# The first pair's 32x32 systems: relaid on chip in place of four hops over DRAM, with a new order of the work

## The chip, the cores and the metric

One core of one Trainium2 chip runs the whole kernel. The metric is device time in microseconds of one execution, as the median of several runs. Engines are called as the profile calls them: PE (TensorE), DVE (VectorE), ACT (ScalarE), POOL (GpSimd), SP (SyncE, which here only issues transfers).

## The reference, cut to what matters

Three parts follow one another on 4 x 768 = 3072 tokens: a delta-rule attention with 8 heads of 48, a rational MLP (called MoE in the code), and eight experts with a capacity of 384 tokens each.

```python
# attention, per batch and head; state is 48x48
k_n = k / (norm(k) + 1e-06)
for t in range(768):
    y[t] = q[t] @ state
    state = state + beta[t] * outer(k_n[t], v[t] - k_n[t] @ state)
# rational MLP on x = y, 3072 x 384
h = x @ w_in                                   # 384 -> 2048
P = a[0] + a[1]*h + a[2]*h**2 + a[3]*h**3
Q = 1.0 + abs(b[0])*abs(h) + abs(b[1])*h**2
x2 = (P / (Q + 1e-06)) @ w_out                 # 2048 -> 384
# experts: greedy assignment of tokens by logits, then per expert
logits = x2 @ w_gate
out[mask] = maximum(x2[mask] @ w1[e], 0) @ w2[e]
```

The weights come in as 64-bit floats; the kernel decodes them to 32 bits on DVE and splits them into two halves of 16 bits.

## The kernel before

**Tiling.** The 768 positions are cut into 12 chunks (NCK) of 64. In a chunk the recurrence becomes a triangular system of 64x64 for each of the 32 heads (two halves of 16, U = 16, on 128 partitions). Each such system is solved in 32x32 blocks: two diagonal blocks and one block below them. Two chunks form a pair: pair 0 is chunks 0 and 1, pair 1 is chunks 2 and 3. A pair has 128 diagonal systems, one on each partition, 32x32 = 1024 numbers in the free dimension.

**How a pair's systems are made.** `gram` computes k k^T on PE into PSUM (tile tg). `gram_k` evacuates it to SBUF (tile ka; for chunk 1 the tile of xs) and writes it to DRAM (dA). `subst` loads it from there in the other layout, one system on a partition (pmA, eight transfers a pair), takes the norms from the diagonal (`root`, `nrec`), and inverts by columns (`col`, two instructions a column: a product into pmT, a subtraction in pmW). For pair 0 the columns run on VectorE and only up to 16x16 (n16: 15 columns on both 16x16 halves at once); the others run on POOL with 31 columns. The result is written to DRAM (dW) and read back by `inv_in` in the first layout (D). `parts` reads from dA the 16x16 blocks below the diagonal (F) and the 32x32 block (P). `merge(c)` completes the 32x32 inverse of a chunk from D and F: two runs of 128 small matmuls (`prod`), a transposition on VectorE, a copy, a subtraction. So the data of pair 0 go over DRAM at four places: dA written, read as pmA and as F and P, dW written, read as D.

**What follows.** The inverse of chunk 0 and P go through `comb`, `comb2`, `tr`, `y` and `pack` and give xT, the input of the MoE part. Each chunk is cut into 8 units: `h` (18 matmuls, line 875, with w_in), `s1`, `s2`, `s3` (the rational function on ACT, DVE and POOL), `x2` (12 matmuls, line 824, with w_out). Units 0 to 15 (chunks 0 and 1) are in the prologue, beside the decode of w_in (`wi_piece`, twelve pieces) and w_out (`wo_piece`, sixteen pieces); the first units need the first column block of w_in, the later ones the others, one after another. From unit 16 on the steady loop runs, then the last chunk, the routing and the experts.

**What sets the order.** `prologue` adds work to a list (`Sched`), each piece with its engine, an estimated time, the names that it reads and writes, and a priority (PP; in the loop LP); a lower priority goes first. `Sched.run` plans the list once, when the program is built, and emits the instructions in the planned order; on the chip every engine takes its instructions in that fixed order and waits by semaphores. All transfers named here are issued by SP, in order. Between the planned matmuls `run` puts warm-up matmuls (`hot`, line 1395) so that PE does not idle.

## Time and profile before

| | |
|---|---|
| time before, median of 3 runs | 968.44 us (965.59 to 973.08) |
| the profiled execution's own time | 968.31 us |
| its span on the core | 966.5 us |
| busy, share of the span | PE 88%, DVE 80%, ACT 58%, POOL 42% |
| DMA, mean over the span | 101 GB/s; 78336 of 101512 packets under 512 B |

The shares are means over stages with different limits, so the rows below are read by stage. Warm-up matmuls count as PE's busy time. A line number is one of the kernel before; "[4.45 <-DMA x]" behind an instruction is the idle time of its engine before it and what ended it. In a row of a stretch the engines stand in the order PE, PEld (weight loads), DVE, ACT, POOL. PEclk is the granted clock of PE as a share of full speed.

### The profile page before, as it was taken

The page shows a single profiled execution, that of the slowest core. Times are in us where ns is not written, and L with a number is a line of the kernel's source. Part 1 is how long each engine was busy: PE and PEld are TensorE (multiplying, and loading weights), DVE is VectorE, ACT ScalarE, POOL GpSimd, SP SyncE. Part 2 cuts the span into 40 slices and gives each one's busy share as a digit, 9 for nine tenths or more (in the row PEclk, how much of TensorE's full clock was granted, in tenths as well). Part 3 has the DMA queues.
Part 4 walks back from the last instruction along what each step waited for, and adds up shares of the span by engine and source line. Part 5 has one row for each costly group of instructions (what it writes and reads, how often), then busy time and mean ns, then how long its engine had stood idle before and what let it go on. Part 6 is the DMA issues. An engine that isn't in the chain of part 4 may idle for free.

```text
span 966.5 us, 30502 instructions
## 1 busy us (share of the span) xinstructions
...
## 2 busy tenths in 40 slices
...
GB/s 305 186 241 121 128 113 113 53 74 23 146 121 52 56 122 100 63 57 156 38 91 51 54 55 1 34 5 14 2 169 159 151 30 196 156 155 128 266 25 24
DMA packets 101512, 97.50 MB, mean 101 GB/s; under 512 B 78336, under 2 KB 86144, under 8 KB 98560
## 3 DMA queue, kind: packets, MB, share of 16 engines
...
q8 instruction: 101, 1.65, 0.8%
...
## 4 chain that ended last, share of the span: by engine, by line
PE 32%; DVE 29%; ACT 11%; DMA 10%; issue 10%; POOL 4%; SPq 3%; POOLq 0%; DVEq 0%; ACTq 0%
PE ph L875 9%; PE eph L770 4%; PE px L824 4%; DVE q L864 3%; DVE w L867 3%; DVE w L868 3%; PE px L783 3%; PE px L1395 3%; DVE w L851 2%; ACT q L858 2%; DVE q L850 2%; DMA xg<-x2d,perm 2%; DVE w L852 2%; ACT w L861 2%; DMA w1f<-in_moe_w_dram,ix 2%
## 5 line engine op out<-in xcount | busy, mean ns | idle before, releaser
L875 PE MATMUL ph<-xT,wi 128*128 128x256 f16 x1656 | 202.7, 278 | 26.4 <-DVE w L851 24.1
L875 PEld LDWEIGHTS <-wi 128*128 128x128 f16 x1728 | 167.0, 100 | 71.5 <-DVE w L851 34.6
L824 PE MATMUL px<-wo,gg 128*128 128x392 f16 (+1 forms) x1116 | 203.5, 333 | 5.2 <-ACT gg L840 2.9
L824 PEld LDWEIGHTS <-gg 128*128 128x128 f16 x1116 | 106.4, 99 | 75.0 <-issue 5.0
L841 POOL TENSOR_TENSOR gg<-w,gg 128x512 f16<-128x512 f32 x59 | 70.5, 1194 | 181.8 <-ACT gg L840 139.4
L188 POOL TENSOR_TENSOR pmW<-pmW,pmT 128x31 f32<-128x31 f32 (+15 forms) x155 | 94.9, 612 | 11.1
L187 POOL TENSOR_TENSOR pmT<-pmW,pmA 128x31 f32<-128x31 f32 (+15 forms) x155 | 86.6, 559 | 11.4
L861 ACT ACTIVATE w<-ph,cf 128x512 f32<-128x512 f32 x88 | 68.2, 775 | 22.8 <-PE ph L875 20.3
L867 DVE TENSOR_TENSOR w<-w,ph 128x512 f32<-128x512 f32 x88 | 59.8, 681 | 22.4 <-ACT q L858 12.2
L852 DVE SCALAR_TENSOR_TENSOR w<-q,w 128x512 f32<-128x512 f32 x88 | 76.5, 869 | 1.3
L840 ACT ACTIVATE gg<-w 128x512 f16<-128x512 f32 x88 | 55.4, 630 | 37.8 <-DVE w L852 37.3
L864 DVE SCALAR_TENSOR_TENSOR q<-q,cf,ph 128x512 f32<-128x512 f32 x88 | 65.1, 740 | 12.4 <-ACT w L861 6.8
L858 ACT ACTIVATE q<-ph,cf 128x512 f32<-128x512 f32 x88 | 60.0, 682 | 23.3 <-PE ph L875 12.7
L783 PEld LDWEIGHTS <-rr 128*128 128x128 f16 x576 | 52.3, 97 | 33.6 <-issue 2.3
L868 DVE SCALAR_TENSOR_TENSOR w<-w,cf,ph 128x512 f32<-128x512 f32 x88 | 65.3, 742 | 9.9 <-ACT q L858 9.4
L1395 PEld LDWEIGHTS <-warm 128*128 128x128 f16 x542 | 54.1, 104 | 24.5 <-issue 10.5
L773 ACT ACTIVATE rr<-eph 128x384 f16<-128x384 f32 x64 | 31.0, 490 | 60.3 <-PE eph L770 52.4
L850 DVE SCALAR_TENSOR_TENSOR q<-q,ph 128x512 f32<-128x512 f32 x88 | 59.8, 680 | 6.9 <-ACT ph L849 6.4
L865 ACT ACTIVATE q<-q 128x512 f32<-128x512 f32 x88 | 55.2, 628 | 16.9 <-DVE q L864 15.9
L851 DVE SCALAR_TENSOR_TENSOR w<-w,cf,ph 128x512 f32<-128x512 f32 x88 | 65.0, 738 | 0.0
L848 ACT ACTIVATE ph<-q,cf 128x512 f32<-128x512 f32 x88 | 60.6, 688 | 6.4 <-DVE ss L103 2.8
L788 POOL DMA_INDIRECT out_dram<-yo,perm x24 | 28.1, 1170 | 81.9 <-ACT yo L785 75.0
...
## 6 DMA issues: line engine op xcount, KB each, us to landing
...
```

The source lines that it names most:

```text
L187: if half==0: eng.tensor_tensor(t,W[:,0:r,j:j+1].to_broadcast([n,r,k]),A[:,j:j+1,j+1:32].to_broadcast([n,r,k]),op=OP.mult)
L188: else: eng.tensor_tensor(W[:,0:r,j+1:32],W[:,0:r,j+1:32],t,op=OP.subtract)
L783: g.add(('PE',.163,lambda P=P,rh=rh,wh=wh,f=f,part=part,i=i: nc.tensor.matmul(P,r[:,rh,f,128*i:128*i+128],W2[:,wh,f],start=(f,part)==(0,0) ...
L824: te.matmul(T['px',un//8][bp][:,0:O.N],gg()[:,gh,i,128*bp:128*bp+128],M.wo[:,wh,fb,0:O.N],start=fb==0 and n==0,stop=fb==15 and n==2,skip_g ...
L851: add(('DVE',.07+.6*z,lambda: ve.scalar_tensor_tensor(w(),w(),cf[:,0:1],y(),op0=OP.add,op1=OP.mult)),W+Y,W,un+O.pd('w3',un))
L852: add(('DVE*',.07+.535*z,lambda: ve.scalar_tensor_tensor(w(),q(),2.0,w(),op0=OP.subtract,op1=OP.mult)),Q+W,W,un+O.pd('w4',un))
L861: ac.activation(w(),P(),AF.Identity,bias=cf[:,2:3],scale=cf[:,3:4])
L864: add(('DVE',.07+.6*z,lambda: ve.scalar_tensor_tensor(q(),q(),cf[:,4:5],P(),op0=OP.add,op1=OP.mult)),Q+Pn,Q,un+O.pd('mu',un))
L867: add(('DVE',.07+.535*z,lambda: ve.tensor_tensor(w(),w(),P(),op=OP.mult)),W+Pn,W,un+O.pd('w1',un))
L868: add(('DVE',.07+.6*z,lambda: ve.scalar_tensor_tensor(w(),w(),cf[:,1:2],P(),op0=OP.add,op1=OP.mult)),W+Pn,W,un+O.pd('w2',un))
L875: for wh,xh in ((0,0),(0,1),(1,0)): te.matmul(T['P',un][:,i],M.wi[:,wh,part,128*fb:128*fb+128],xT()[:,xh,part],start=n==0,stop=n==8); n+=1
L1395: for _ in range(n): nc.tensor.matmul((bk['px1'] if t is None else t)[:,0:256],warm[:,0:128],warm,start=True,stop=True)
```

## The change

For pair 0 only, the four passages over DRAM go.

- `gram_0` replaces `gram_k` for chunks 0 and 1. The gram of chunk 0 goes to tg, that of chunk 1 to rec. Four evacuations a chunk (32 partitions each, 512 numbers, on ACT or DVE as the planner chooses) write the diagonal blocks of both chunks into one tile G (128x1024), with 32 numbers between neighbours; one stream transposition of G on VectorE gives pmA.
- F and P are evacuated from PSUM by ACT (`off`, four a chunk, scaled by s.odd, which is 1 on the partitions of the odd 16-row blocks and 0 elsewhere; `top`, two a chunk). s.odd is made by one small reduction at the start. `parts` and `inv_in` go.
- At the end of `subst` a second stream transposition, strided on both sides, writes the inverses of both chunks into one new tile nd (nd0, nd1), which replaces h4 and n0 as D.
- The planner's constants PP and LP are all new (cut here to those that the text speaks of).

```diff
--- before.py
+++ after.py
@@ -57,6 +57,7 @@
         nc.vector.tensor_scalar(s.ident,jp,0.0,None,op0=OP.is_equal)
         s.id16=c.tile([128,128],F16,name="id16"); nc.vector.tensor_copy(s.id16,s.ident)
         s.mask=c.tile([128,1,64],F32,name="mask")
+        s.odd=c.tile([128,1],F32,name="odd"); nc.vector.tensor_reduce(s.odd,s.ident.rearrange("t (a b x) -> t a b x",b=2,x=16)[:,:,1],axis=AX.XY,op=OP.add)
 
         s.dA=[[dr.tile([128,U,64],F32,name=f"dA{i}{j}") for j in range(2)] for i in range(2)]
         s.dW=[dr.tile([2,2,2,U,32,32],F32,name=f"dW{i}") for i in range(2)]
@@ -110,9 +111,9 @@
         eng.tensor_tensor(t,t,n[:,u,None].to_broadcast([128,u.stop-u.start,48]),op=OP.mult)
 
 
-    def gram(s,a,x,sw):
+    def gram(s,a,x,sw,pool=None):
         nc=s.nc
-        g=s.tg.tile([128,2,8,64],F32,name="tg")
+        g=(pool or s.tg).tile([128,2,8,64],F32,name="tg")
         for p in range(8):
             if s.mid and p%3==2: s.mid()
             for z in range(2):
@@ -121,12 +122,22 @@
                     t=64*(h^(sw*(p//4))); nc.tensor.matmul(g[t:t+64,r,p],a[o,p,h],x[o,p,h],start=True,stop=True)
         return g
 
-    def gram_k(s,c,ka=None):
+    def gram_0(s,c,P,F):
+        nc=s.nc; k=s.kT[c]; g=s.gram(k,k,0,s.rec if c else s.tg)
+        def out(i,act=True):
+            o=slice(32*i,32*i+32); b=32*(i%2); y=s.G.rearrange("t (x c p r) -> t c r p x",x=32,c=2,p=8)[o,c]; x=g[o,:,:,b:b+32]
+            if act: nc.scalar.activation(y,x,AF.Copy)
+            else: nc.vector.tensor_copy(y,x)
+        def off(i): o=slice(32*i,32*i+32); b=32*(i%2); nc.scalar.activation(F[o].rearrange("t (p r) x -> t r p x",r=2)[:,:,:,0:16],g[o,:,:,b:b+16],AF.Copy,scale=s.odd[o])
+        def top(h): o=slice(64*h,64*h+32); nc.scalar.activation(P[o].rearrange("t (p r) x -> t r p x",r=2),g[o,:,:,32:64],AF.Copy)
+        s.pend+=[lambda act=True,i=i: out(i,act) for i in range(4)]+[lambda i=i: off(i) for i in range(4)]+[lambda h=h: top(h) for h in range(2)]
+
+    def gram_k(s,c):
         nc=s.nc; k=s.kT[c%4]
         g=s.gram(k,k,0)
-        t=[ka]
+        t=[None]
         def out(act=True):
-            if ka is None: t[0]=s.wk.tile([128,U,64],F32,name="ka")
+            t[0]=s.wk.tile([128,U,64],F32,name="ka")
             o=t[0].rearrange("t (p r) x -> t r p x",r=2)
             if act: nc.scalar.activation(o,g,AF.Copy)
             else: nc.vector.tensor_copy(o,g)
@@ -147,26 +158,19 @@
         for u in range(U):
             for q in range(4): o=slice(32*q,32*q+32); s.nc.tensor.matmul(out[o,u],a[o,u],x[o,u],start=True,stop=True)
 
-    def parts(s,m,e,F,X):
-        nc=s.nc; x=s.dA[m%2][e]
-        for h in range(2):
-            for b in range(2): o=64*h+32*b; nc.sync.dma_start(F[o+16:o+32,:,0:16],x[o+16:o+32,:,32*b:32*b+16])
-            nc.sync.dma_start(X[64*h:64*h+32],x[64*h:64*h+32,:,32:64])
-    def inv_in(s,m,e,D):
-        for h in range(2):
-            for b in range(2): o=64*h+32*b; s.nc.sync.dma_start(D[o:o+32],s.dW[m%2][h,b,e].rearrange("u j i -> j u i"))
-
-    def subst(s,m,eng,n16=False):
+    def subst(s,m,eng,n16=False,D=None):
 
         nc=s.nc; n=128; x={}; ss=s.ss[m%2]; z=[]
         def load(c):
             if not x: x.update(A=s.wk.tile([128,1056],F32,name="pmA"),W=s.wk.tile([128,1056],F32,name="pmW"),T=s.wk.tile([128,256],F32,name="pmT"))
-            for h in range(2):
+            for h in range(2) if c is not None else ():
                 for b in range(2):
                     o=64*h+32*b+16*c; q=64*h+32*b
                     nc.sync.dma_start(f3(x['A'])[o:o+16],s.dA[m%2][c][q:q+32,:,32*b:32*b+32].rearrange("j u i -> u j i"))
         f3=lambda t: t[:,0:1024].rearrange("p (a b) -> p a b",b=32); f4=lambda t: t.rearrange("p (y z) -> p y z",y=2)[:,:,0:512].rearrange("p y (a b) -> p y a b",b=32)[:,:,:,0:16]
-        z+=[lambda: load(0),lambda: load(1)]
+        def sys():
+            load(None); nc.vector.transpose(x['A'][:,0:1024],s.G)
+        z+=[sys] if n16 else [lambda: load(0),lambda: load(1)]
         n2=lambda: x['A'][:,0:1024:33]
         z.append(lambda: s.root(ss,n2()))
         z+=[lambda j=j: s.nrec(ss,n2(),s.bp[:,32*m:32*m+32],j) for j in range(7)]
@@ -187,7 +191,8 @@
             if half==0: eng.tensor_tensor(t,W[:,0:r,j:j+1].to_broadcast([n,r,k]),A[:,j:j+1,j+1:32].to_broadcast([n,r,k]),op=OP.mult)
             else: eng.tensor_tensor(W[:,0:r,j+1:32],W[:,0:r,j+1:32],t,op=OP.subtract)
         z+=[lambda j=j,h=h: col(j,h) for j in range(15 if n16 else 31) for h in range(2)]
-        z.append(lambda: (nc.sync if n16 else nc.gpsimd).dma_start(s.dW[m%2].rearrange("h b c u j i -> (h b c u) (j i)"),x['W'][:,0:1024]))
+        if n16: z.append(lambda: nc.vector.transpose(D.rearrange("p (n i) -> p i n",i=32),x['W'][:,0:1024].rearrange("p (j i) -> p i j",i=32)))
+        else: z.append(lambda: nc.gpsimd.dma_start(s.dW[m%2].rearrange("h b c u j i -> (h b c u) (j i)"),x['W'][:,0:1024]))
         return z
 
     def diag_in(s,c):
@@ -964,82 +969,82 @@
...
-    c0=[-2281.9,2107.92],
-    m1=-0.6,
-    gk=[910.4,-4699.67,-1180.67,-8338.9,528.37,-1855.44,2054.53],
-    sub=-1280.78,
+    c0=[2026.08,485.39],
+    m1=1117.59,
+    gk=[-10353.25,1356.37,5016.44,-3988.65,608.84,-1294.95,-1534.33],
+    sub=3666.65,
...
-    wi=1580.99,
-    wc=2548.48,
-    wo=-88.48,
-    p12=-11583.26,
+    wi=4697.11,
+    wc=-28529.46,
+    wo=-751.59,
+    p12=-5159.67,
...
-    GP1=3,
+    GP1=2,
...
-    tol=0.02,
-    wg=-55441.22,
-    wgf=2770.9,
+    tol=0.3,
+    wg=1251.49,
+    wgf=-4090.52,
...
-LP=dict(tol=0.15,
+LP=dict(tol=0.02,
...
 ONE=True
 D_={k: {} for k in ('vm','kl','gk','gq','K','v','q')}
 def PW(k,c): return D_[k][c] if c in D_[k] else PP[k][c]
-def prologue(g,A,M,xT,yev,pack,stg,stx,bk,kb):
+def prologue(g,A,M,xT,yev,pack,stg,stx,bk):
 
     nc=A.nc; te,ac,ve,po,sp=nc.tensor,nc.scalar,nc.vector,nc.gpsimd,nc.sync; T={}
     g.act={}
@@ -1075,8 +1080,8 @@
     def vm(c):
         for h in range(2): add(('POOL*',.87,lambda h=h: A.vmul(c,po,slice(8*h,8*h+8))),[('nt',c//2%2),('V',c%2)],[('V',c%2)],PW('vm',c))
     def GK(c):
-        m=c//2; p=PW('gk',c); ka='kb' if c==1 else 'ka'
-        gk=lambda: A.gram_k(c,kb if c==1 else None); b=mm(2.4 if c<4 else 1.3,warm(gk) if c<4 else gk,['tg'],[('kT',c%4)],TG,p,act=2800 if c<4 else 1536)
+        m=c//2; p=PW('gk',c); ka='ka'
+        gk=lambda: A.gram_k(c); b=mm(2.4 if c<4 else 1.3,warm(gk) if c<4 else gk,['tg'],[('kT',c%4)],TG,p,act=2800 if c<4 else 1536)
         ev(b,0,'ACT',.97,TG,[ka],p)
         add(('SP',(1,1.5),lambda: b[1]()),[ka],[('dA',m%2,c%2)],p)
     def GQ(c):
@@ -1085,8 +1090,9 @@
         ev(b,0,'DVE',1.14,TG+['mk'],['kq'],p)
     def sub_pair(m,pr):
 
-        n16=m==0; e,en=(ve,'DVE*') if n16 else (po,'POOL*'); z=A.subst(m,e,n16); X=[('pm',0),('pm',1)]; S=('ss',m%2); K=15 if n16 else 31; f=(lambda n: dv(n)+.03) if n16 else pc
-        for c in range(2): add(('SP',(4,1.5),z[c]),[('dA',m%2,c)],[X[c]],pr)
+        n16=m==0; e,en=(ve,'DVE*') if n16 else (po,'POOL*'); z=A.subst(m,e,n16,T.get('nd')); z=z[:1]+z if n16 else z; X=[('pm',0),('pm',1)]; S=('ss',m%2); K=15 if n16 else 31; f=(lambda n: dv(n)+.03) if n16 else pc
+        if n16: add(('DVE',1.4,z[1]),[('g0',c,i) for c in range(2) for i in range(4)]+['ka'],X,pr)
+        for c in range(0 if n16 else 2): add(('SP',(4,1.5),z[c]),[('dA',m%2,c)],[X[c]],pr)
         add(('ACT',.25,z[2]),X,[S],pr)
         for j in range(7): add(('DVE*',.2 if j==4 else .11,z[3+j]),(X if j==0 else [])+[S,'bp'],[S],pr)
         add(('DVE*',.13,z[10]),[S],[('nt',m%2)],pr)
@@ -1094,7 +1100,8 @@
         for j in range(K):
             d=f((j+1)*(K-j)*(2 if n16 else 1))
             for h in range(2): add((en,d,z[12+2*j+h]),X,X,pr,chain=PP['pch'])
-        add(('SP',(1,1.5),z[12+2*K]) if n16 else ('POOL',1.1,z[12+2*K]),X,[('dW',m%2)],pr,post=0.0 if n16 else 3.0)
+        if n16: add(('DVE',1.4,z[12+2*K]),X,['nd0','nd1'],pr)
+        else: add(('POOL',1.1,z[12+2*K]),X,[('dW',m%2)],pr,post=3.0)
     add(('POOL',1.6,lambda: po.memset(A.TT,0.0)),[],TD,PP['ms'])
     add(('POOL',.5,A.mask1),[],['mk0'],PP['m1']); add(('DVE',.1,A.mask2),['mk0'],['mk'],PP['m1'])
     for n,w in (('rec',RE),('tg',TG)): add(('DVE',1.15,lambda n=n: ve.memset(bk[n],0.0)),[],w,PP['m1'])
@@ -1103,27 +1110,33 @@
     add(('SP',(1,.3),A.load_beta),[],['bp'],PP['be'])
     for c in range(4): kl(c)
     add(('SP',(2,.2),M.load_ab),[],['ab'],PP['ab'])
-    CH=[dict(B='h1',C='h2',D='h4',F='Ut0',P='Ut1',b=('P0','P1')),dict(B='q1',C='q0',D='n0',F='n2',P='n1',b=('px0','px1'))]
-    for i in range(3): T['n%d'%i]=M.ws.tile([128,512],F32,name='n%d'%i)
+    CH=[dict(B='h1',C='h2',D='nd0',F='Ut0',P='Ut1',b=('P0','P1')),dict(B='q1',C='q0',D='nd1',F='n2',P='n1',b=('px0','px1'))]
+    for i in range(1,3): T['n%d'%i]=M.ws.tile([128,512],F32,name='n%d'%i)
+    T['nd']=M.ws.tile([128,1024],F32,name='nd'); T['nd0'],T['nd1']=T['nd'][:,0:512],T['nd'][:,512:1024]
+    A.G=A.wk.tile([128,U,64],F32,name="ka").rearrange("t u x -> t (u x)")
+    def GK0(c):
+        x=CH[c]; f,pp=x['F'],x['P']; p=PW('gk',c); B_=RE if c else TG
+        add(('POOL',.7,lambda: po.memset(flat(f),0.0)),[],[f],PP['ms'])
+        b=mm(2.4,warm(lambda: A.gram_0(c,sl(pp),sl(f))),['rec' if c else 'tg'],[('kT',c)],B_,p,act=2800)
+        for i in range(4): ev(b,i,'AD',.55,B_,[('g0',c,i)]+['ka'][:c==i==0],p)
+        for i in range(4): ev(b,4+i,'ACT',.4,B_,[f],p+1)
+        for h in range(2): ev(b,8+h,'ACT',.55,B_,[pp],p+2)
     pb=dict(P0=P2(0),P1=P2(1),px0=[('px',0)],px1=[('px',1)])
     def merge(c):
         x=CH[c]; p=PP['c0'][c]; b_,c_,d,f,pp=[x[n] for n in 'BCDFP']; b0,b1=x['b']; pv=lambda b: view(bk[b],[128,U,32])
-        add(('POOL',.7,lambda: po.memset(flat(f),0.0)),[],[f],PP['ms'])
-        add(('SP',(6,1.2),lambda: A.parts(0,c,sl(f),sl(pp))),[('dA',0,c)],[f,pp],p)
-        add(('SP',(4,1.2),lambda: A.inv_in(0,c,sl(d))),[('dW',0)],[d],p)
         add(('PE',2.6,lambda: A.prod(pv(b0),sl(f),sl(d))),[f,d],pb[b0],p,act=512)
         add(('DVE',.7,lambda: ve.transpose(sl(c_),sl(d))),[d],[c_],p)
         add(('ACT',.6,lambda: ac.activation(sl(b_),pv(b0),AF.Copy)),pb[b0],[b_],p)
         add(('PE',2.6,lambda: A.prod(pv(b1),sl(c_),sl(b_))),[b_,c_],pb[b1],p,act=512)
         add(('DVE',.63,lambda: ve.tensor_tensor(sl(d),sl(d),pv(b1),op=OP.subtract)),pb[b1]+[d],[d],p)
     c0=PP['c0'][0]
-    GK(0); GK(1); sub_pair(0,PP['c0'][0]); merge(0)
-    def tn(): t=A.st[0,'tn']=A.wk.tile([128,U,32],F32,name="tn"); ve.transpose(t,sl('h4'))
-    add(('DVE',.7,tn),['h4'],['tn'],c0)
+    GK0(0); GK0(1); sub_pair(0,PP['c0'][0]); merge(0)
+    def tn(): t=A.st[0,'tn']=A.wk.tile([128,U,32],F32,name="tn"); ve.transpose(t,sl('nd0'))
+    add(('DVE',.7,tn),['nd0'],['tn'],c0)
     def ttd(k,e):
-        o=32*k; c=o%64; y=lambda: A.TT[o:o+32,:,c:c+32]; x=lambda: sl('h4')[o:o+32]
+        o=32*k; c=o%64; y=lambda: A.TT[o:o+32,:,c:c+32]; x=lambda: sl('nd0')[o:o+32]
         return (lambda: ac.activation(y(),x(),AF.Copy)) if e=='ACT' else (lambda: po.tensor_copy(y(),x()))
-    for k in (1,3,0,2): add([('ACT',.55,ttd(k,'ACT')),('POOL',1.0,ttd(k,'POOL'))],['h4'],[('TT',k)],c0)
+    for k in (1,3,0,2): add([('ACT',.55,ttd(k,'ACT')),('POOL',1.0,ttd(k,'POOL'))],['nd0'],[('TT',k)],c0)
     def a12(): A.st[0,'A12']=sl('Ut1'); A.comb(0)
 
     def lows(t,hi,lo,sc,n,pool,S,wh,wl,p):
@@ -1169,7 +1182,7 @@
         def go(): A.y(c,yev); A.ds(c)
         last=c==NCK-1
         b=mm(1.1 if last else 2.1,(lambda: A.y(c,yev)) if last else go,['rec'] if last else ['rec','tg'],UT+['kq']+(RE if c else [])+([] if last else [('Kn',c%2)]),RE if last else RE+TG,P,act=1024 if last else 2048)
-        ev(b,0,'ACT',.97,RE,['xs']+(['kb'] if c==0 else []),P); ev(b,1,'DVE',1.2,RE+['xs'],['xl'],P)
+        ev(b,0,'ACT',.97,RE,['xs'],P); ev(b,1,'DVE',1.2,RE+['xs'],['xl'],P)
         if c==0: ev(b,2,'ACT',.8,TG,['Sb'],P)
         elif not last: ev(b,2,'DVE',.87,TG+['Sb'],['Sb'],PP['st%d'%c][5])
     def pk(c,pr): add(('SP',(6,1.5),lambda: pack(c)),['xs','xl','cf'],[('xT',c%2),'xs'],pr)
@@ -1384,7 +1397,7 @@
             ws=pro.enter_context(tc.tile_pool(name="mws",bufs=1,side="right"))
             M.ws=ws; stx=ws.tile([128,FF//2,2],I32,name="wsi")
             stg=[M.wk.tile([128,512],F32,name=n,bufs=b) for n,b in (("sa",2),("sa",2),("q",2),("q",2),("w",3),("w",3),("w",3),("y",2),("y",2))]
-            xT['s']=xw.tile([128,2,1024],F16,name="xs",bufs=1); kb=xT['s'].rearrange("p a t -> p (a t)").bitcast(F32).rearrange("p (u j) -> p u j",j=64); bk={}
+            xT['s']=xw.tile([128,2,1024],F16,name="xs",bufs=1); bk={}
             for n,pool in (("tg",tg),("rec",rec)):
                 bk[n]=pool.tile([128,1024],F32,name=n)
                 for i in range(2): bk["%s%d"%(n,i)]=bk[n][:,512*i:512*i+512]
@@ -1395,7 +1408,7 @@
                 for _ in range(n): nc.tensor.matmul((bk['px1'] if t is None else t)[:,0:256],warm[:,0:128],warm,start=True,stop=True)
             hot(H00)
             g=Sched(); g.nc=nc; g.tol=PP['tol']; g.free.update(SP=0.6,POOL=3.2,DVE=2.5,ACT=2.0,PE=2.5)
-            g.x2d,g.Lt=x2d,Lt; g.mid=lambda: hot(2); T,i1=prologue(g,A,M,xT,yev,pack,stg,stx,bk,kb); i0=next(i for i,t in enumerate(g.t) if t[0][0][0]=='PE'); i1=max(i for i in range(len(g.t)) if g.t[i][0][0][0]=='PE')
+            g.x2d,g.Lt=x2d,Lt; g.mid=lambda: hot(2); T,i1=prologue(g,A,M,xT,yev,pack,stg,stx,bk); i0=next(i for i,t in enumerate(g.t) if t[0][0][0]=='PE'); i1=max(i for i in range(len(g.t)) if g.t[i][0][0][0]=='PE')
             run(g,hot,i0,i1,0,HM,HG,[(('px',1),bk['px1'])]+[(b,bk[b]) for b in ('tg0','tg1','rec0','rec1')])
         rc=ctx.enter_context(tc.tile_pool(name="rc0",bufs=1,side="right"))
         def route():
```

## Rows read from the trace of the kernel before

**Rows 1.** Stretches: start:end length, busy us (instructions) by engine; PEclk, DMA share, GB/s
```profile
0.00:110.00 110.00, 86.65 (x1746) 69.69 (x1748) 66.34 (x147) 28.05 (x48) 35.60 (x57) 0.84 0.77 211
110.00:231.00 121.00, 103.75 (x1879) 79.16 (x1872) 101.94 (x176) 80.53 (x144) 80.48 (x146) 0.94 0.33 79
231.00:617.00 386.00, 359.02 (x6936) 264.12 (x6937) 337.30 (x497) 299.06 (x502) 198.52 (x275) 0.99 0.31 74
```

**Rows 2.** Stretches of line 875 alone (unit matmuls): PE, PEld, then as above
```profile
300.00:350.00 50.00, 18.81 (x162) 15.37 (x163) 1.00 0.28 79
```

**Rows 3.** Chain that ended last, first stage: start us, us, what
```profile
18.69 8.55 DMA vn<-in_v_dram
...
48.28 6.12 DMA kt<-in_k_dram
```

**Rows 4.** Stretches of 5 us, columns as in rows 1
```profile
5.00:10.00 5.00, 5.00 (x29) 3.72 (x28) 0.55 (x2) 0.00 (x0) 0.00 (x0) 1.00 0.97 386
...
25.00:30.00 5.00, 5.00 (x49) 4.47 (x47) 4.03 (x7) 1.49 (x3) 0.00 (x0) 1.00 1.02 141
```

**Rows 5.** DMA packets of the first 110 us
```profile
DMA packets 25822, 23.17 MB, mean 211 GB/s; under 512 B 20526, under 2 KB 21037, under 8 KB 25037
```

**Rows 6.** SP's issues in order: start us, us of issue, line, out<-in, count
```profile
21.90 9.46 SPq L167 DMA_DIRECT2D pmA<-dA  x8
...
31.98 2.04 SPq L153 DMA_DIRECT2D ut<-dA  x2
...
44.27 0.61 SPq L154 DMA_DIRECT2D n<-dA  x1
...
49.76 0.38 SPq L190 DMA_DIRECT2D dW<-pmW  x1
...
60.93 3.55 SPq L157 DMA_DIRECT2D wo<-dW  x4
...
67.65 3.21 SPq L157 DMA_DIRECT2D n<-dW  x4
```

**Rows 7.** Instructions of the systems in order: start us, us, engine, line, out<-in
```profile
11.23 0.46 PE L121 MATMUL tg<-kt 48*64 48x64 f32 x16
13.42 1.02 ACT L131 ACTIVATE ka<-tg 128x1024 f32<-128x1024 f32 x1 [11.18 <-PE tg L121]
...
16.79 1.02 ACT L131 ACTIVATE xs<-tg 128x1024 f32<-128x1024 f32 x1 [2.34 <-PE tg L121]
...
35.66 0.35 ACT L94 ACTIVATE ss<-pmA,tiny 128x32 f32<-128x32 f32 x1 [7.77 <-DMA pmA<-dA]
...
39.02 0.60 DVE L177 COPY pmW<-ss 128x32 f32<-128x32 f32 x1
...
40.99 0.19 DVE L184 TENSOR_TENSOR pmW<-pmW,pmT 128x30 f32<-128x30 f32 x1
...
49.18 0.21 DVE L184 TENSOR_TENSOR pmW<-pmW,pmT 128x30 f32<-128x30 f32 x1
...
54.53 0.70 PE L121 MATMUL tg<-kt 48*64 48x64 f32 x16 [7.90 <-DMA kt<-in_k_dram]
...
66.28 0.71 DVE L1115 STREAM_TRANSPOSE wo<-wo 128x512 f32<-128x512 f32 x1 [3.04 <-DMA wo<-dW]
```

**Rows 8.** Unit matmuls on PE in order of time (units 0, 8, 9, 16)
```profile
110.69 4.09 PE L875 MATMUL ph<-xT,wi 128*128 128x256 f16 x36
...
157.77 2.78 PE L875 MATMUL ph<-xT,wi 128*128 128x256 f16 x24
180.50 2.12 PE L875 MATMUL ph<-xT,wi 128*128 128x256 f16 x9
...
230.95 3.77 PE L875 MATMUL ph<-xT,wi 128*128 128x256 f16 x18 [2.58 <-DVE w L851]
```

**Rows 9.** Evacuations of 32x512 from PSUM by line: ns min/median/max, times, shape
```profile
L232 ACT ACTIVATE tt<-rec x18: 570/580/590, 92.3 to 579.6; 32x512 f32<-32x512 f32 x18
L233 DVE TENSOR_SCALAR tt<-rec x6: 672/689/690, 93.0 to 547.5; 32x512 f32<-32x512 f32 x6
```

92 lines of the change are left out of this document (46 added, 46 removed).

## The prediction

> **What bounds the kernel now.** I read the stages first (busy time by stretch), then the chain that ended last, then SyncE's queue and the DMA share, and only then single instructions. The span falls into three parts that matter here [rows 1]. In the first 110 us no MoE unit runs; PE is busy because it is fed warm-up matmuls, while VectorE works 66.3 us of the 110. Units 0 to 15 run from 110 to 231, with VectorE busy 84% of the time. From 231 to 617 the steady loop runs with VectorE at 87% and PE at 93%: 162 unit matmuls, nine units, in 50 us [rows 2], 5.6 us a unit, or 5.4 over its 72 units, against 7.5 us for units 0 to 15. So the loop is near a bound of two engines, while the first stage is bound by a chain; what is saved there is kept by all that follows as long as the loop keeps its pace.
>
> The chain in the first stage goes through SyncE and its transfers: it stands 8.6 us behind one load and 6.1 us behind another [rows 3]. The reader is to see that these are not slow single loads. Between 25 and 30 us the DMA engines are fully busy (1.02) and move 141 GB/s; between 5 and 10 us they are as busy (0.97) and move 386 GB/s [rows 4]. What lies between is the kind of packet: of 25822 packets in the first 110 us, 20526 are under 512 B [rows 5], and SyncE takes 9.46 us to issue the eight loads of the systems alone [rows 6].
>
> The systems' own path, by its instructions: the evacuation of the second gram starts at 16.79 and takes 1.02, so both grams are in SBUF at 17.81; the root, the first step that needs the relaid systems, starts at 35.66; the last column ends at 49.39; the inverse is back for chunk 0 at 66.28 [rows 7]. So 17.9 us go to the hop in, 13.7 us to the substitution, 16.9 us to the hop out. The first unit starts at 110.69 [rows 8], 44.4 us after that.
>
> **Part 1: the hop in.** Removed are two writes of dA, eight loads of pmA and twelve of the parts. The second gram now has banks of its own (rec), so it no longer waits for the evacuation of tg: a gram with its fillers takes 2.2 us (the first, from 11.23 to its evacuation at 13.42 [rows 7]), so the second ends near 15.6, where its evacuation now starts at 16.8. Eight evacuations of 32x512 replace the two large ones; the nearest rows are 0.58 us on ScalarE and 0.69 us on VectorE [rows 9]. The first four run beside the second gram; the last four, on two engines, end at 15.6 + 2x0.69 = 17.0; all eight on ScalarE would end at 13.4 + 8x0.58 = 18.1. The first stream transposition has 1024 columns; the one of 512 takes 0.71 [rows 7], so 1.42. That is 18.6 to 19.7 with the waits; I take 19.5 for the root, against 35.66. While the transposition waits for the last evacuation, decode pieces of the weights stand behind it on VectorE, at most 2 us, and ScalarE's conversions stand behind the evacuations.
>
> The parts F and P now cost ScalarE eight evacuations of 256 (between the 0.35 of the root's 32 elements [rows 7] and 0.58; I take 0.45) and four of 512: 3.6 + 2.3 us. With four of the first eight, less the two old ones, that adds 6.2 us to a ScalarE that is busy 28.1 of 110 us [rows 1]. That idle time is the cover; without it 6.2 us. They hold tg and rec to about 25 us, and no other gram stands before 54.5 in the old order [rows 7], so nothing waits. The small reduction for s.odd falls before the first load has landed. Both cost nothing.
>
> **Part 2: the strided copies.** The evacuations write every 32nd element (128 B apart); the second transposition reads and writes so. No row shows it for 512 elements. From below: the first and the last column both write 30 elements, the first one in a run, the last one 128 B apart, and take 0.19 and 0.21 us [rows 7]. That is 0.7 ns an element, 0.7 us for a transposition of 1024. From above: the copy to the diagonal, 32 elements 132 B apart, takes 0.60 us against the 0.19 of the first column's 30 [rows 7]: 12.8 ns an element, 13.1 us for 1024. I take 0.7 ns, because that row is a chain of dependent VectorE work like ours, and the copy stands right behind a long memset of the same tile. The Trainium skill, page "SBUF — State Buffer", section "Door 1: The DMA port swizzle", says that SBUF has lines of 16 bytes and that each access that crosses to a new line pays a penalty, so four fp32 are the longest free stride. It names no size; the 0.21 against 0.19 agrees with a small one, the 0.60 with a large one, and by the large one the sum below would turn into a loss (rival 3).
>
> **Part 3: the hop out.** Removed are the write of dW and eight loads. The substitution keeps its 13.7 us: 19.5 + 13.7 = 33.2. The second transposition takes 1.42 + 0.7 = 2.1: D of both chunks is there at 35.3, against 66.28. The path to the first chunk's inverse gets 31.0 us shorter.
>
> **Part 4: what SyncE and the DMA engines get back.** Thirty-one transfers go. SyncE's rows for them sum to 27.4 us of issue between 14 and 71 us (the loads of pmA 9.5, eight rows of parts 10.1, two of the inverse 6.8, three writes 1.0 [rows 6]). In packets: 8x512 for pmA, 8x256 and 4x512 for the parts, 8x512 for the inverse, 12288 of the 20526 small ones. Queued behind them on SyncE were loads of q, v, the keys of chunk 3 and w_in; they come earlier. The bytes before the first unit, 23.2 MB, would take 60 us at 386 GB/s, so DMA does not forbid a first unit at 80.
>
> **Part 5: the new order.** In the constants the systems go from -2282 to 2026 (c0), behind the w_out pieces (-752) and ahead of the w_in pieces (4697); lower goes first. So columns may be interleaved with decode, and D may come later than 35.3; what VectorE decodes meanwhile is then done. It is therefore counted as a balance of VectorE. Before the first unit it did 66.3 us [rows 1]. The change adds 2x1.42 + 4x0.69 = 5.6, in all 72. With the 44.4 us after D unchanged the first unit starts at 35.3 + 44.4 = 79.7, near 31 us sooner. VectorE would have to be busy 90% from the start; between the 60% of this stage and the 87% of the loop I take 81%, so 64 us are done and 8 us of decode go over into units 0 to 15. VectorE has 19 us idle there [rows 1]; if these hide all, 0 is lost, if none, 8, and at 76% 12. I take 8.
>
> Sum: 31 - 8 = 23 us. The profiled span is 966.5 us, its run 968.3 and the median 968.44, so they stand as one. 966.5 - 23 + 1.8 = **945 us**. A check from the other side: VectorE's work up to unit 16, 66.3 + 101.9 + 5.6 = 173.9 us, at the loop's 87.4% takes 199 us against 231, so 32 us is the most that this part gives without a better order than the loop's.
>
> **The rivals.**
> 1. *VectorE's decode becomes the bound.* The first stage's chain is shorter, but w_in's and w_out's pieces end no sooner than 95 to 100 us, as they are queued behind late loads; the first unit gains 11 to 16 us and units 0 to 15 give back some. Gain 5 to 12: 956 to 963. For it: VectorE has 72 us to do; against: it was idle for 44 us of 110.
> 2. *The new order also closes later holes.* Unit 8 is fed at 157.8, unit 9 only at 180.5 [rows 8]. If a third to a half of that goes too, the gain is 33 to 42 us: 926 to 935. The balance above speaks against it.
> 3. *Strided copies at 12.8 ns an element.* Place: an evacuation then takes 0.69 + 6.5 = 7.2 us, four on each engine, so the last one ends at 13.4 + 28.8 = 42.2; the first transposition reads and writes in runs, the root starts at 44, the last column ends at 58, and the second transposition takes 1.4 + 13.1, so D comes at 72, 6 us later than before. VectorE has 39 us more to do, and at the same 81% it has 17 us of decode left when the first unit starts, of which the 19 us of idle time may hide half: 6 + 8 = 14 us slower, 981. It decides where 3072 elements, one behind another on this path, eat the 23 us: at 7.5 ns an element. For it the 0.60 us row; against it the 0.21 us row.
> 4. *The loop loses by its new constants.* LP is all new. If PE's busy share in it goes from 93% to 90%, the 386 us become 399: 13 of the 23 us are lost, 958.
> 5. *The change does not do what it says in time*: the columns stand behind so much decode that the inverse comes no sooner than 60: 963 to 972.
>
> **How the numbers follow.** The forecast 0.60 (its own range 936 to 954), rival 1 0.15, rival 2 0.08, rival 3 0.06, rival 4 0.08, rival 5 0.03. The range 932 to 963 takes in the forecast, rival 1 and rival 4, and leaves out most of rivals 2, 3 and 5: about 0.17. About 1% is what a measurement of this kernel tells from no change, here 959 and 978. Faster: 0.60, rival 2, a third of rival 1, half of rival 4, some 0.76. Slower: rival 3 and a little, 0.07. Within 1%: 0.17.
>
> **What would show it.** Right: no dW from pmW on SyncE; the root near 20, the second transposition between 33 and 45, each transposition under 2.5 us; the DMA share clearly under 1 between 25 and 45 us; the first unit matmul at 75 to 86; unit 16 at 200 to 216; 72 units of the loop still 5.4 us each. Wrong: evacuations of 32x512 over 1 us (part 2); the first unit later than 90 with VectorE busy throughout (rival 1) or waiting for a DMA (part 4); the loop longer than 395 us (rival 4).

## The result, and the profile after

The changed kernel takes 943.5 us (median, 942.95 to 947.0), the kernel before, run beside it, 969.9: a ratio of 0.9738 [0.9691, 0.9785], 26 us faster. The forecast was 945. The profiled execution took 943.24 us, its span 941.2. What follows asks whether the working was as right as its sum. It was not.

The stages of the kernel after, cut at the first unit, unit 16, the end of the loop and the routing (columns as in [rows 1]):

```profile
0.00:93.44 93.44, 67.16 (x1643) 54.15 (x1644) 71.01 (x146) 37.03 (x63) 27.19 (x44) 0.83 0.68 207
93.44:222.00 128.56, 108.64 (x1899) 83.97 (x1900) 106.34 (x177) 81.93 (x148) 73.50 (x109) 0.93 0.31 76
222.00:598.30 376.30, 355.36 (x6873) 264.12 (x6874) 341.16 (x507) 299.26 (x502) 212.30 (x319) 1.00 0.31 77
598.30:680.50 82.20, 65.04 (x534) 43.71 (x532) 60.05 (x130) 44.31 (x77) 18.60 (x33) 0.92 0.04 11
680.50:941.20 260.70, 238.01 (x1891) 147.33 (x1887) 205.28 (x741) 110.73 (x249) 73.40 (x88) 0.97 0.37 135
```

The same cuts of before are 110.69, 120.26, 386.05, 83.0 and 266.5 us long. So the first stage gained 17.3 us, units 0 to 15 lost 8.3, the loop gained 9.8, the last chunk and the routing 0.8, the experts 5.8: 25.3 in all. The forecast had 31, a loss of 8, and nothing from the rest.

Where units start, for [rows 8] (units 0, 8, 10 and 16; TensorE's timeline):

```profile
93.44 2.72 PE L880 MATMUL ph<-xT,wi 128*128 128x256 f16 x12 [2.37 <-DMA xT<-xs]
...
156.19 2.13 PE L880 MATMUL ph<-xT,wi 128*128 128x256 f16 x18
...
184.47 0.49 PE L880 MATMUL ph<-xT,wi 128*128 128x256 f16 x3
...
221.94 2.13 PE L880 MATMUL ph<-xT,wi 128*128 128x256 f16 x18
```

The hole that stood between units 8 and 9 is still there, now ahead of unit 10. Unit 16 comes 9.0 us sooner, not 15 to 31.

The path of the systems, for [rows 7] (timelines of ScalarE, VectorE, POOL and TensorE put together in order; L129 and L130 are the evacuations on ScalarE and VectorE, L131 one of those that make F, L172 and L194 the two transpositions, L95 the root, L181 the copy to the diagonal, L187 and L188 columns, L111 a scaling of v on POOL, L159 the first product with the inverse, L1408 warm-up):

```profile
12.00 1.04 ACT L129 ACTIVATE ka<-rec 32x512 f32<-32x512 f32 x1 [9.76 <-PE rec L122]
...
13.07 1.03 DVE L130 COPY ka<-rec 32x512 f32<-32x512 f32 x1 [5.47 <-ACT ka L129]
...
14.14 2.18 ACT L129 ACTIVATE ka<-rec 32x512 f32<-32x512 f32 x2 [0.78 <-DVE ka L130]
...
19.89 1.03 DVE L130 COPY ka<-tg 32x512 f32<-32x512 f32 x1
...
20.95 2.10 ACT L129 ACTIVATE ka<-tg 32x512 f32<-32x512 f32 x2
23.08 1.05 DVE L130 COPY ka<-tg 32x512 f32<-32x512 f32 x1 [2.17 <-ACT ka L129]
24.16 0.47 ACT L131 ACTIVATE ut<-tg,odd 32x256 f32<-32x256 f32 x1 [1.11 <-DVE ka L130]
...
24.50 1.24 DVE L172 STREAM_TRANSPOSE pmA<-ka 128x1024 f32<-128x1024 f32 x1
...
28.15 0.33 ACT L95 ACTIVATE ss<-pmA,tiny 128x32 f32<-128x32 f32 x1
...
31.98 1.62 POOL L111 TENSOR_TENSOR vn<-vn,nt 128x384 f32<-128x384 f32 x2 [4.02 <-DVE nt L177]
...
33.05 0.60 DVE L181 COPY pmW<-ss 128x32 f32<-128x32 f32 x1
33.33 6.94 PE L1408 MATMUL px<-warm 128*128 128x256 f16 x62
...
35.16 0.19 DVE L188 TENSOR_TENSOR pmW<-pmW,pmT 128x30 f32<-128x30 f32 x1
...
42.08 1.63 POOL L111 TENSOR_TENSOR vn<-vn,nt 128x384 f32<-128x384 f32 x2 [8.47 <-DMA vn<-in_v_dram]
42.27 0.75 DVE L187 TENSOR_TENSOR pmT<-pmW,pmA 128x78 f32<-128x78 f32 x1
...
44.58 0.21 DVE L188 TENSOR_TENSOR pmW<-pmW,pmT 128x30 f32<-128x30 f32 x1
...
45.30 1.91 DVE L194 STREAM_TRANSPOSE nd<-pmW 128x1024 f32<-128x1024 f32 x1
47.36 1.93 PE L159 MATMUL px<-nd,n 32*32 32x32 f32 x128 [7.08 <-DVE nd L194]
```

Three things are to be seen. The eight evacuations take 1.03 to 1.10 us each, and none runs beside another: where one engine follows the other within a chunk, it starts 0.03 us after the other's evacuation has ended. The transposition ends at 25.74, but the root starts only at 28.15: ScalarE has evacuations and conversions of its fixed order in front of it. And the inverse is there at 47.2, 19.1 us sooner than before (66.28), where 31.0 were forecast. The waits of that stretch name the first (engine, line, waited for: us in total, times, longest):

```profile
DVE ka L130 <- ACT ka L129: 7.6, 2, 5.5
```

Of the longest of these waits, 5.5 us, only the last 1.04 are the turn itself; before 12.00 the gram was not there. The turns go at least with the tile in PSUM that both engines read: at 24.16 ScalarE's first evacuation of F, which reads tg and writes another tile than ka, waits for VectorE's too, while at 20.37 one that reads rec runs beside VectorE's of tg.

What SyncE and the DMA engines got back, for [rows 4] and [rows 5] (two stretches of 5 us; the packets of the first 110 us):

```profile
25.00:30.00 5.00, 4.99 (x96) 3.83 (x94) 4.36 (x9) 4.55 (x12) 1.94 (x3) 1.00 0.75 305
...
35.00:40.00 5.00, 5.00 (x48) 4.47 (x46) 4.49 (x20) 0.00 (x0) 0.00 (x0) 1.00 0.99 387
...
DMA packets 13075, 21.50 MB, mean 195 GB/s; under 512 B 7808, under 2 KB 8320, under 8 KB 12288
```

From 25 to 30 us the DMA engines now move 305 GB/s at a share of 0.75, where they moved 141 at 1.02. The share is not clearly under 1 all the way from 25 to 45 us, as the prediction had it: it is 0.91 from 30 to 35 and 0.99 from 35 to 40. Over the whole run 12784 packets under 512 B are gone (78336 to 65552), close to the 12288 counted in the prediction.

### The profile page after: what moved, and what is told of

It reads as the page before. It is cut to its first block, busy times and chain, and to the rows that moved or that the text cites. A ratio compares the mean times of both kernels' runs of the same rounds, so it can differ in the third digit from the quotient of the medians.

```text
span 941.2 us, 30209 instructions
## 1 busy us (share of the span) xinstructions
PE 834.2 (89%) x12831; PEld 593.3 (63%) x12831; DVE 783.9 (83%) x1698; ACT 573.3 (61%) x1037; POOL 405.0 (43%) x590
## 2 busy tenths in 40 slices
DMA packets 88343, 94.47 MB, mean 100 GB/s; under 512 B 65552, under 2 KB 73360, under 8 KB 85392
## 4 chain that ended last, share of the span: by engine, by line
PE 35%; DVE 29%; ACT 13%; issue 10%; DMA 8%; SPq 2%; POOL 2%; POOLq 0%; DVEq 0%; ACTq 0%
PE ph L880 9%; PE eph L775 6%; PE px L829 5%; PE px L788 3%; DVE q L869 3%; DVE w L872 3%; ACT q L863 2%; DVE w L873 2%; ACT w L866 2%; DMA dA<-ka 2%; DMA xg<-x2d,perm 2%; DVE w L856 2%; DVE w L857 2%; DVE q L855 1%; DMA w2f<-in_moe_w_dram,ix 1%
## 5 line engine op out<-in xcount | busy, mean ns | idle before, releaser
L880 PE MATMUL ph<-xT,wi 128*128 128x256 f16 x1656 | 200.6, 276 | 22.0 <-DVE q L855 15.0
L829 PE MATMUL px<-wo,gg 128*128 128x392 f16 (+1 forms) x1116 | 201.0, 330 | 3.6 <-ACT gg L845 2.6
L846 POOL TENSOR_TENSOR gg<-w,gg 128x512 f16<-128x512 f32 x54 | 63.6, 1178 | 160.1 <-ACT gg L845 129.3
L191 POOL TENSOR_TENSOR pmT<-pmW,pmA 128x31 f32<-128x31 f32 (+15 forms) x155 | 92.5, 597 | 11.4
L872 DVE TENSOR_TENSOR w<-w,ph 128x512 f32<-128x512 f32 x88 | 59.6, 680 | 16.4 <-ACT q L863 12.1
L788 PEld LDWEIGHTS <-rr 128*128 128x128 f16 x576 | 52.3, 97 | 32.4 <-issue 2.0
L870 ACT ACTIVATE q<-q 128x512 f32<-128x512 f32 x88 | 55.4, 630 | 15.6 <-DVE q L869 14.3
L775 PE MATMUL eph<-xe,w1s 128*128 128x384 f16 x288 | 55.8, 340 | 1.0 <-ACT xe L766 1.0
```

What stands on the lines that cost most here:

```text
L191: if half==0: eng.tensor_tensor(t,W[:,0:r,j:j+1].to_broadcast([n,r,k]),A[:,j:j+1,j+1:32].to_broadcast([n,r,k]),op=OP.mult)
L775: g.add(('PE',.163,lambda P=P,wh=wh,xh=xh,j=j,f=f,part=part: nc.tensor.matmul(P,W1[:,wh,f,j],xe[:,xh,j],start=(part,j)==(0,0),stop=(part,j ...
L788: g.add(('PE',.163,lambda P=P,rh=rh,wh=wh,f=f,part=part,i=i: nc.tensor.matmul(P,r[:,rh,f,128*i:128*i+128],W2[:,wh,f],start=(f,part)==(0,0) ...
L829: te.matmul(T['px',un//8][bp][:,0:O.N],gg()[:,gh,i,128*bp:128*bp+128],M.wo[:,wh,fb,0:O.N],start=fb==0 and n==0,stop=fb==15 and n==2,skip_g ...
L872: add(('DVE',.07+.535*z,lambda: ve.tensor_tensor(w(),w(),P(),op=OP.mult)),W+Pn,W,un+O.pd('w1',un))
L880: for wh,xh in ((0,0),(0,1),(1,0)): te.matmul(T['P',un][:,i],M.wi[:,wh,part,128*fb:128*fb+128],xT()[:,xh,part],start=n==0,stop=n==8); n+=1
```

## Experiments

The theory is a chain: in a given order the first unit follows pair 0's inverse at a fixed distance, and all that comes later follows the first unit. The rivals are that other work (decode, the order) sets the first unit, or that the time comes from the constants alone. As a mark behind loop and routing serves the first load of an expert's weights: 706.62 before, 687.15 after. All ratios are to the kernel before, run beside each kernel.

| kernel | inverse there | first product with it | first unit | first expert load | time, us | ratio |
|---|---|---|---|---|---|---|
| after | 47.2 | 47.36 | 93.44 | 687.15 | 943.5 | 0.9738 [0.9691, 0.9785] |
| dup | 57.0 | 57.13 | 102.66 | 696.86 | 957.2 | 0.9868 [0.9828, 0.9907] |
| hop_out | 54.5 | 54.54 | 102.33 | 698.39 | 957.5 | 0.9821 [0.9776, 0.9867] |
| hop_in | 49.8 | 49.94 | 95.62 | 690.56 | 950.7 | 0.9774 [0.9731, 0.9816] |
| runs | 45.7 | 45.83 | 91.47 | 686.14 | 944.9 | 0.9725 [0.9683, 0.9767] |
| front_act | 44.9 | 45.03 | 90.99 | 684.65 | 946.3 | 0.9721 [0.9678, 0.9765] |
| front_root | 42.3 | 42.43 | 87.91 | 680.71 | 945.8 | 0.9744 [0.9705, 0.9783] |
| nocols | 38.2 | 40.42 | 85.85 | 677.38 | 939.0 | 0.9681 [0.9642, 0.9719] |
| early | 34.0 | 41.79 | 86.36 | 679.24 | 939.0 | 0.9676 [0.9647, 0.9705] |

In hop_out six of the 128 small products start between 53.15 and 54.54, as their loads land.

### Constants and data path, taken apart

Four kernels cross the two data paths (hops, relaid on chip) with the two sets of constants. PP orders the prologue, LP the loop.

```diff
 # relay_oldPPLP: the changed kernel
-PP=dict(K=[2081.9,2098.33,...  and LP=dict(tol=0.02, ...      # its own
+PP=dict(K=[7339.93,4085.14,... and LP=dict(tol=0.15, ...      # those of before
 # hops_newPPLP: the kernel before, with both sets of the changed one
 # relay_oldLP, hops_newLP: LP alone exchanged
```

> The changed kernel with both tables of constants (PP, LP) of the kernel before: the relay without the new order. If the shorter path itself brings the gain (path theory), the second transposition ends near 45 us, the first unit starts 15 to 20 us sooner than the 110.7 of before, and the time is 945 to 955 us. If the new constants bring it (order theory), the time is 962 us or more. If the gain is a sum of 9 us before unit 16, 10 us in the loop and 6 us in the experts (sum theory), the loop from unit 16 on takes 386 us as before and the time is 953 to 960.

> The kernel before, hops over DRAM and all, with both tables of constants of the changed kernel: the new order without the relay. Path theory: 966 to 972 us, since the inverse still comes back near 66 us or later. Order theory: 945 to 955. Sum theory: the loop takes 376 us, the first unit starts near 110, and the time is 955 to 962.

> The changed kernel with the loop's constants (LP) of the kernel before; the prologue's plan is untouched, so the first unit starts at 93.4 and unit 16 at 222 as in the changed kernel. Sum theory: the loop takes 386 us instead of 376, the time is about 953. Path theory: the loop's length follows from the state in which the prologue leaves the engines, the time stays at 943.5.

> The kernel before with the loop's constants (LP) of the changed kernel; its prologue's plan is untouched, so the first unit starts at 110.7 and unit 16 at 231. Sum theory: the loop takes 376 us instead of 386, the time is about 960. Path theory: 969.

Measured: relay_oldPPLP 1026.4 us, ratio 1.0554 [1.0515, 1.0592]; hops_newPPLP 1010.2, 1.0389 [1.0350, 1.0429]; relay_oldLP 966.5, 0.9953 [0.9920, 0.9985]; hops_newLP 964.4, 0.9945 [0.9915, 0.9976]. So each data path with the other's constants is 40 to 57 us slower than before, and only the pair of both is faster by more than half a per cent. None of the theories foresaw this: hops_newPPLP is 38 us above the highest of its figures, relay_oldLP 13 us above, and relay_oldPPLP fits only the open end of the order theory. Whether a new fit of the constants on the old data path would gain something was not tried. The data path alone did what it says: in relay_oldPPLP the inverse is there at 44.4. But the old order then spends the gain in places where it had assumed other end times (timelines of TensorE and VectorE):

```profile
87.28 1.21 DVE L153 TENSOR_TENSOR kq<-tg,mask 128x1024 f32<-128x1024 f32 x1
88.60 2.04 PE L255 MATMUL tg<-vn,tt 64*64 64x48 f32 x64 [20.65 <-issue]
...
194.79 1.93 DVE L317 TENSOR_SCALAR wof<-wst 128x384 int32<-128x384 int32 x2 [36.50 <-POOL wo L1148]
```

TensorE stands 20.7 us in front of a product of chunk 0 that writes tg, until VectorE has evacuated kq from that tile at 88.49, behind a row of decode pieces; the first unit comes only at 102.35, 57.9 us behind the inverse. In hops_newPPLP it comes 36.4 us behind it (80.7 and 117.07). So the distance from inverse to first unit is no fixed one; it goes with the order and the data path that it meets. In relay_oldPPLP VectorE also stands 36.5 us in front of a piece of w_out that waits for POOL behind pair 2's last column. That is an order made for other durations.

LP alone: on the changed path the old LP costs 23 us by the medians (21 by the ratios), on the old path the new LP gains 5. The first unit is where the changed kernel has it (93.42), so the loss lies behind it; the first expert load, from POOL's timeline, in after:

```profile
687.15 1.10 POOL L722 DMA_INDIRECT w1f<-in_moe_w_dram,ix  x1 [12.17 <-DVE ic L643]
```

The same view of relay_oldLP:

```profile
703.55 1.10 POOL L722 DMA_INDIRECT w1f<-in_moe_w_dram,ix  x1 [11.70 <-DVE ic L643]
```

From first unit to first expert load it is 610 us with the old LP and 594 with the new one; before took 596. The loop's gain in the stage table thus comes with the new LP: 16 us of this profile, 21 to 23 of the time. Counted by the unit matmuls, the 72 units from unit 16 on take 390.5 us in after and 408.9 in relay_oldLP, 400.4 in before and 396.4 in hops_newLP; so the new LP is worth 18 us behind the new prologue and 4 behind the old one.

### The inverse made late and early

```diff
 # dup: the second transposition six times over
-if n16: z.append(lambda: nc.vector.transpose(D...,x['W']...))
+if n16: z.append(lambda: [nc.vector.transpose(D...,x['W']...) for _ in range(6)])
 # nocols: pair 0's 30 column instructions left out
 def col(j,half):
+    if n16 and j<15: return
```

> The changed kernel with its order kept and the final transposition into nd done six times instead of once: 5 x 1.91 = 9.6 us more on VectorE right ahead of the inverse, which then comes at about 57 instead of 47. Chain theory: the first unit starts at 103 and the time is 953. Balance theory: the same 9.6 us, since they are VectorE's work too. If there is slack behind the first unit (slack theory: the hole between units 9 and 10 ends at 184 whatever comes before), the first unit is late by 9.6 but unit 16 and the time only by 0 to 4: 943 to 948.

> The changed kernel with its order kept, the thirty column instructions of pair 0 left out (so the inverse of the first pair is not computed): 8 us less on VectorE right ahead of the inverse, which then comes at about 38.5 instead of 47. Chain theory and balance theory: the first unit at 85, the time 935. Slack theory: the first unit sooner by 4 to 8, unit 16 and the time by 0 to 3: 940 to 944.

VectorE's and TensorE's timelines in dup:

```profile
45.36 11.62 DVE L194 STREAM_TRANSPOSE nd<-pmW 128x1024 f32<-128x1024 f32 x6
57.13 1.93 PE L159 MATMUL px<-nd,n 32*32 32x32 f32 x128 [16.79 <-DVE nd L194]
102.66 2.72 PE L880 MATMUL ph<-xT,wi 128*128 128x256 f16 x12 [2.22 <-DMA xT<-xs]
```

TensorE's timeline in nocols:

```profile
33.55 6.94 PE L1409 MATMUL px<-warm 128*128 128x256 f16 x62
40.42 1.29 PE L159 MATMUL px<-nd,n 32*32 32x32 f32 x128
...
85.85 2.72 PE L881 MATMUL ph<-xT,wi 128*128 128x256 f16 x12 [1.75 <-DMA xT<-xs]
```

The inverse 9.8 us later moves the first unit by 9.2 and the first expert load by 9.7; the time rises by 13.7 (medians) or 12.6 (ratios). The inverse 9.0 sooner moves them by 7.6 and 9.8; the time falls by 4.5 or 5.5. The chain holds in the profile both ways. The time does not follow one for one: it rose by more than the inverse was late, and fell by about half of what it was early (953 and 935 were expected, 957.2 and 939.0 came). In nocols the inverse is there at 38.2, but its first product starts at 40.42, directly behind 62 warm-up matmuls.

### One relay taken back at a time

```diff
 # hop_out: the second transposition replaced
-nc.vector.transpose(D...,x['W']...)
+nc.sync.dma_start(s.dW[0]...,x['W'][:,0:1024])     # one write
+nc.sync.dma_start(d[o:o+32],s.dW[0][h,b,e]...)     # eight loads
 # hop_in: the strided evacuations and the first transposition replaced
-nc.scalar.activation(y,x,AF.Copy) / nc.vector.tensor_copy(y,x)   # eight of 32x512
+nc.scalar.activation(k_...,g,AF.Copy); nc.sync.dma_start(s.dA[0][c],k_)   # one a chunk
-load(None); nc.vector.transpose(x['A'][:,0:1024],s.G)
+load(0); load(1)                                   # eight loads
```

> The changed kernel with the second transposition alone taken back: pair 0's solved systems go over DRAM again (one write, eight loads), the first relay stays on chip, the plan is kept. Chain theory (the first unit, and with it the end, follows the pair's inverse one for one): the inverse comes 10 to 17 us after the 47.2 of the changed kernel, at 57 to 64, the first unit at 104 to 110, the time 954 to 962. Rival (the second hop was hidden behind the planned work anyway): first unit within 2 us of 93.4, time 943.5 to 946.

> The changed kernel with the first relay alone taken back: the Gram matrices are evacuated whole, one to a chunk, written to DRAM and loaded as systems (eight loads), in place of eight strided evacuations and the first transposition; the second relay stays on chip, the plan is kept. Chain theory: the root comes 8 to 15 us after the 28.15 of the changed kernel, and the first unit as much after 93.4; time 953 to 962. If the eight strided evacuations cost nearly as much as the hop (they took some 11 us of the chain with their waits): root within 3 us of 28.15 and 942 to 947.

SyncE and TensorE in order, in hop_out:

```profile
45.68 0.33 SPq L195 DMA_DIRECT2D dW<-pmW  x1
48.32 4.06 SPq L199 DMA_DIRECT2D nd<-dW  x8
54.54 1.91 PE L159 MATMUL px<-nd,n 32*32 32x32 f32 x122 [0.38 <-DMA nd<-dW]
```

ScalarE and SyncE in order, in hop_in:

```profile
18.44 1.02 ACT L131 ACTIVATE ka<-tg 128x1024 f32<-128x1024 f32 x1
22.65 4.85 SPq L170 DMA_DIRECT2D pmA<-dA  x8
30.95 0.35 ACT L95 ACTIVATE ss<-pmA,tiny 128x32 f32<-128x32 f32 x1 [7.38 <-DMA pmA<-dA]
```

The second relay is worth 7.3 us of the inverse (54.5 against 47.2) and 8 (ratios) to 14 us (medians) of the time. The expectation (57 to 64) was too high, as the hop took only 8.9 us here, from 45.65. The first relay is worth 2.6 us: the root comes 2.8 us later, as the rival had it (within 3); the time of 950.7 lies between the two expectations, by the ratios 3.5 us above after, with intervals that overlap. Eight evacuations of 1.04 in series, their gaps and a root held up on ScalarE cost nearly what the hop costs. Both together, 9.9 us, are half of the 19.1 by which the inverse comes sooner. The other half is that a hop itself is shorter in this kernel. In before, from the second gram's evacuation to the root took 18.9 us, here (hop_in) 12.5; the eight loads took SyncE 9.46 us to issue [rows 6], here 4.85. From the last column to the inverse took 16.9 us, as SyncE came to the loads 11.2 us after the write [rows 6]; here it comes 2.6 after it. How this half divides between the new order and the parts' twelve loads that are gone was not taken apart; the order alone does not give it, since in hops_newPPLP the inverse came at 80.7.

### The front of the chain

```diff
 # runs: evacuations write runs of 32, the first transposition reads strided instead
-y=s.G.rearrange("t (x c p r) -> t c r p x",x=32,...)
+y=s.G.rearrange("t (c p r x) -> t c r p x",x=32,...)
-nc.vector.transpose(x['A'][:,0:1024],s.G)
+nc.vector.transpose(x['A'][:,0:1024].rearrange("p (x n) -> p x n",n=32),s.G.rearrange("t (n x) -> t x n",x=32))
 # front_act: runs, and
-if act: nc.scalar.activation(y,x,AF.Copy)
+if act or c==0: nc.scalar.activation(y,x,AF.Copy)     # chunk 0: ScalarE only
+...                       # chunk 1's off/top issued behind chunk 0's; memset of pmW on POOL, early
 # front_root: front_act, but all off/top except two issued behind the root and init
 # early: front_root without pair 0's columns, as in nocols
```

> The changed kernel with its order kept: the eight evacuations into G write runs of 32 numbers, and the first stream transposition reads with a stride of 32 numbers instead. If the stride is what makes an evacuation 1.04 us, each falls to 0.58 on ScalarE and 0.69 on VectorE, the first transposition rises from 1.24 to about 1.9, and the root starts about 2.5 to 3 us sooner than 28.15. Chain theory (the time follows the inverse's arrival one for one): 940.5 to 941.5 us. Balance theory (VectorE's work up to unit 16 sets the end): 1.4 us less work on VectorE, 942. If the 0.5 us are something else than the stride, nothing moves.

> The changed kernel with runs of 32 written by the evacuations (the first transposition reads strided instead), all four evacuations of the second chunk to come put on ScalarE and ahead of the first chunk's other two evacuations, and the zeroing of the transposition's target moved to GpSimd. Expected: the first transposition starts at 20 instead of 24.50, the inverse is there at 42.4 instead of 47.2. Chain theory: first unit at 88 to 89, time 938 to 941. Rival (slack behind the inverse takes it, or the loop gives it back as its plan was fitted to the old front): 943 to 945.

> As the run before it (runs of 32, the second chunk's evacuations all on ScalarE and ahead, zeroing on GpSimd), but the root of the first pair's system norms is put on ScalarE ahead of eight of the evacuations to P and F, which waited in front of it and kept the root at 27.43 where its transposition had ended at 22.37; they now run behind the next two conversions of w_in. Expected: root at 22.4 to 23, the columns 3 to 4 us sooner than there, the inverse at 41 (47.2 in the changed kernel, 44.9 in the run before). Chain theory: first unit 87 to 88, first expert load 681 to 683, time 936 to 941. Rival (what is gained ahead of the first unit is given back in the loop, whose plan was fitted to where the first pair left the engines): first unit as above, but the first expert load at 685 to 687 and the time at 943 to 947.

> The kernel of the run before (root ahead on ScalarE) with pair 0's 30 column instructions left out (pair 0's systems are not solved, so the output is not the reference's): it moves the inverse as early as this order allows, to 31 to 34 (47.2 in the changed kernel, 42.3 in the run before, 38.2 where the columns alone were left out). It tells whether the first unit still follows the inverse there, or whether the decode of w_in or another cover sets it. Chain theory: first unit 45.6 to 47.6 after the inverse, as in the runs so far, at 77 to 81; first expert load 671 to 676; time 930 to 936. Rival (decode bound, the first rival of the prediction): first unit at 84 or later, the gap behind the inverse at 51 us or more, time 938 or more.

ScalarE and VectorE in runs:

```profile
13.44 0.59 ACT L129 ACTIVATE ka<-rec 32x512 f32<-32x512 f32 x1 [11.20 <-PE rec L122]
14.05 0.68 DVE L130 COPY ka<-rec 32x512 f32<-32x512 f32 x1 [6.22 <-ACT ka L129]
...
22.81 1.95 DVE L172 STREAM_TRANSPOSE pmA<-ka 128x1024 f32<-128x1024 f32 x1
```

Written in runs an evacuation takes 0.59 us on ScalarE and 0.68 on VectorE instead of 1.04 and 1.03; the transposition pays, 1.95 instead of 1.24. The engines still take turns (0.59 after 13.44 is 14.03, and VectorE starts at 14.05), so the turns are not the stride's doing. The root comes at 26.44, 1.7 us sooner, where 2.5 to 3 were expected; the inverse gains 1.5 us, the time nothing that can be told.

VectorE and ScalarE in front_act:

```profile
20.43 1.94 DVE L179 STREAM_TRANSPOSE pmA<-ka 128x1024 f32<-128x1024 f32 x1 [1.18 <-ACT ka L129]
...
27.43 0.34 ACT L95 ACTIVATE ss<-pmA,tiny 128x32 f32<-128x32 f32 x1
```

ScalarE, VectorE and TensorE in front_root:

```profile
22.03 0.35 ACT L95 ACTIVATE ss<-pmA,tiny 128x32 f32<-128x32 f32 x1
...
40.37 1.91 DVE L201 STREAM_TRANSPOSE nd<-pmW 128x1024 f32<-128x1024 f32 x1
42.43 1.28 PE L163 MATMUL px<-nd,n 32*32 32x32 f32 x128 [1.47 <-DVE nd L201]
```

front_act misses its number (42.4) by 2.5 us: its transposition ended at 22.37, yet the root came at 27.43, because the evacuations that had been moved out of the way of the transposition now stood in front of the root (eight of them and two conversions ran after 22.37). With them behind it (front_root) it starts at 22.03, the inverse is there at 42.3, the first unit at 87.91, the first expert load at 680.71, all as the chain theory said (the inverse 1.3 us late, the unit on the mark). The time does not show it: 945.8, from 939.86 to 948.19, and the profiled execution was the fastest of them. That median is the rival's (943 to 947); the late expert load by which the rival explained it is not in the profile. So neither is a version that is shown to beat the changed kernel; the 5 us that the profile of front_root shows are about what the intervals of two ratios, 0.4% either way each, can hide.

TensorE and VectorE in early:

```profile
32.07 1.96 DVE L202 STREAM_TRANSPOSE nd<-pmW 128x1024 f32<-128x1024 f32 x1
...
34.91 6.94 PE L1416 MATMUL px<-warm 128*128 128x256 f16 x62
41.79 1.29 PE L163 MATMUL px<-nd,n 32*32 32x32 f32 x128
...
86.36 2.72 PE L888 MATMUL ph<-xT,wi 128*128 128x256 f16 x12 [0.40 <-DMA xT<-xs]
```

The inverse is there at 34.0, and the first unit comes 52.3 us later, at 86.4: the chain theory's 77 to 81 is missed, and so are its 930 to 936 us; the distance, the unit and the time (939.0, as in nocols) are those that the rival named. But the rival's cause, the decode, is not what the trace shows: the first product stands behind the same 62 warm-up matmuls until 41.79, from there to the first unit it is 44.6 us, as in all kernels of the table (44.6 to 47.8), and what the unit waits for last is its input xT. The first unit has a floor in this order, and it is the filler put between two planned steps of TensorE. That taking it out would help is not shown. In after, where TensorE had stood idle for 7.1 us, the 128 first products took 1.93 us at a granted clock of 0.50 (the level of 1.2 GHz); in early, right behind the fillers, 1.29 at 1.00.

## Why the sum was right and its terms were not

**The mechanism held.** The first unit follows the inverse: 46.2 us after it, where 44.4 were taken over from before; no dW from pmW stands on SyncE any more; the packets fell as counted; each transposition took under 2.5 us (1.24 and 1.91 against 1.42 and 2.1). The other signs of "right" failed: the root, the second transposition (done at 47.2, not between 33 and 45), the first unit (93.44, not 75 to 86) and unit 16 came late, and the DMA share was near 1 from 30 to 40 us. A first unit later than 90 was a sign of "wrong" for rival 1, but the other half of that sign did not come: VectorE was not busy throughout before it (71.0 of 93.4 us).

**That the sum came out is luck.** 31 became 17.3, the loss of 8 became 8.3, and the zero for all that follows became 16.4: 25.3 where 23 were forecast, as one error of 14 us and one of 16 cancelled.

**Part 1 failed: the root at 19.5 came at 28.15.** The prediction had evacuations of 0.58 and 0.69 us on two engines side by side. They took 1.04 and ran one after another. Part 2 had the right price in hand, 0.7 ns an element for a stride of 128 B, and did not apply it where it matters: 512 elements of it are 0.36 us, which makes 0.94 and 1.05 out of 0.58 and 0.69. The turns were not thought of at all. The Trainium skill comes near them: its page "PSUM — Partial Sum Buffer", section "PSUM bank collisions raise a hardware error", says that two engines must not be on the same bank and the same quarter of the partitions at once, and that the simple guard goes by bank. The four evacuations of a chunk read the same banks from different quarters; the trace shows that the program orders them all the same (the waits above). Whether they could run side by side was not tried. But stride and turns together are not the largest part of the 8.7 us. Chunk 0's gram stands on TensorE behind 30 warm-up matmuls and ends 1.8 us later than the 15.6 of the prediction; its first evacuation, at 19.89, stands 2.5 us more behind pieces of decode on VectorE; the four evacuations take 4.24 us instead of 1.4, 2.8 more; a piece of decode, 0.4; the transposition is 0.2 shorter; and the root waits 2.4 us for ScalarE instead of the 1.1 allowed, 1.3 more. Two thirds are thus order. That last wait is a term which the prediction put at nothing: the evacuations to F and P had ScalarE's idle time as their cover, and six of them, with two conversions, stood in front of the root.

The sign named for "wrong", evacuations over 1 us, came true without rival 3: the stride costs 0.9 ns an element on ScalarE and 0.7 on VectorE (worked out from runs), far from 12.8 and from the 7.5 that would decide. The Trainium skill's rule (page "SBUF — State Buffer", section "Door 1: The DMA port swizzle") that crossing to a new line of 16 bytes pays a penalty agrees with that; it gives no size, the runs do. The copy to the diagonal, the row with 12.8, took 0.60 again. Its price is neither the stride nor, as the prediction guessed, the place behind the memset, but POOL: the copy started while POOL was at the second of two products that scale v and ended 0.05 us behind it (33.60 and 33.66). In front_root POOL began 0.1 us after the copy, and the same copy to the same places took 0.20; in hops_newPPLP, behind the same memset, it ran beside a longer product of POOL's and took 0.93, again until 0.05 us behind it. So the prediction chose the right one of two prices, for a reason that was not the cause.

**Part 3 failed by 3 us more.** From the root to the end of the last column it is 16.6 us instead of 13.7. Of the 30 column instructions 28 kept their durations (0.19 and 0.21 at both ends); two, which started while POOL was at a scaling of v, took 0.75 each instead of 0.24, 1.0 us together. The other 1.9 are pieces of decode that stand in between in the new order. Together 8.7 + 2.9 + 0.5 of waiting - 0.2 of the transposition are the 11.9 us by which the inverse missed 35.3. And 35.3 could not have been used: the 62 warm-up matmuls would have held its first product to about 40.3 (33.33 + 6.94).

**Part 5 was right in size and wrong in cause.** Units 0 to 15 lost 8.3 us, 8 were forecast. But the forecast was decode left over because the first unit comes early: 64 us done before it. VectorE did 71.0 there, nearly all of the 72 (which count the second transposition at 1.42 and not at the 2.1 of part 3). And what is left over would shrink with a later first unit; yet from first unit to unit 16, counted by matmuls, it is 126 us in nocols (first unit 85.8), 127 in hop_in (95.6) and 128 in hop_out (102.3). So the loss goes with the new order of the units, not with the balance; the hole ahead of unit 10 is part of it. What in that order costs the 8 us stays open.

**The zero for the loop was wrong, and covered the miss.** 9.8 us came from the loop. Rival 4 had weighed a loss by the new LP; it was a gain, and on this data path a large one (relay_oldLP). Unit 16 at 222 instead of 200 to 216 and units of 5.2 us (376.3 / 72) instead of 5.4 say the same.

**The experts' 5.8 us are not claimed for the change.** Their code is untouched, and from first expert load to the end of the span the profiles of all these kernels scatter from 254.1 (after) to 260.4 (front_act), with 259.9 in before. Some of the 26 us is therefore open: 19.5 lie between the start and the first expert load (17.3 + 2.2), the rest is in a part where single executions differ by as much.
